# Bulk loads of four batches in two parts of uneven row counts

## The chip, the cores and the metric

One core of one Trainium2 chip. The metric is the device time of one execution in microseconds; lower is better.

## The reference

An attention layer followed by a mixture of experts, all in float32. 8 batches, 8 heads, 512 local and 32 global tokens of width 64.

```python
s_g = scale * np.matmul(q_g, k_all.transpose(0, 1, 3, 2))      # global queries see all keys
out_g = np.matmul(sm(s_g), v_all)
s_ll = np.where(np.abs(pos[:, None] - pos[None, :]) <= 32, scale * q_l @ k_l^T, -1e9)
a_l = sm(concat([scale * q_l @ k_g^T, s_ll]))                  # local queries: a window and the global keys
out_l = np.matmul(a_l, concat([v_g, v_l]))
x = concat([out_g, out_l]) as 4352 rows of 512
expert_idx = argmax(xn @ en.T / tau)                           # each row goes to one of 8 experts
out[mask] = gate_w[mask] * (np.maximum(x[mask] @ w1[e], 0.0) @ w2[e])
```

(Abridged; `sm` is a softmax. `w1` is 512 x 1024 and `w2` 1024 x 512 for each expert.)

## The kernel before

**Data as it is loaded.** The host lays out the queries and keys of a batch as `qk[b]`, 128 rows of 4 x 1216 floats (`RW` = 1216): rows 0 to 63 are heads 0 to 3, rows 64 to 127 heads 4 to 7, and the four pieces `j` of a row are the head pairs. The values are `va[b]`, two head groups of 128 rows of 14 windows of 4 x 65 floats. Rows are the partitions of the on-chip tiles `raw` (two buffers, one batch each) and `vt` (six buffers, one step each).

**Steps.** The attention stage runs in 32 steps `g`, four per batch, and two more to drain; `slot(g)` emits one. A step takes 128 local queries of all heads. In one slot the code emits, in this order: the scores of step `g` (line 415, reads `raw`), the transposes of the probabilities of `g-1` (462), the masked maxima of `g` (432, VectorE), the exponentials (451, ScalarE), the values of `g-2` (477, reads `vt`), norms, and pieces of the routing (turning the rows of `x`, logits, the choice of the expert, and a scatter of the rows to DRAM, line 730, by GpSimd's queue). The global queries of a batch are done in between (512 to 575). The order on each engine is the order of the code.

**Bulk loads.** `load(b, j, k)` (259 to 264) issues one half of one piece of a batch's `raw`: 128 rows of 608 floats, 304 KB. `load_v(g, n)` (266 to 275) issues a quarter of a step's `vt`: 128 rows of up to two windows of one head group, 260 KB, or 130 KB where a step has only three windows (`VCUT`; steps 0 and 3 of a batch). All go through SyncE's queue. The loads of `vt` for step `g` are handed out in slot `g`; those of `raw` for batch `b` in slots `4b-5` to `4b-2`, two per slot (lines 862 to 868). So steps 10, 14, 18 and 22 carry the last piece (`j` = 3) of batches 3, 4, 5 and 6, which the scores of steps 12, 16, 20 and 24 are the first to read.

**Pace.** A slot's list of loads is cut in two halves that are interleaved (878 to 881). With six loads, v0 to v3 and k0, k1, the order is v0, v3, v1, k0, v2, k1. `tick(ins, part)` (245 to 250) is called at six places of a slot, behind chosen instructions of VectorE and ScalarE, and issues from the list until its share of `part`/6 is reached; each load issued there waits for that instruction (`paced`, 231 to 240):

```python
while parts and share[0] * 6 < part * share[1]:
    parts.pop(0)()
    share[0] += 1
```

The six places are the first maximum, the copy of the turned probabilities (467), three exponentials (451) and the copy of the turned rows (596).

**Expert stage.** From about 290 us on, 36 and more blocks of 128 rows go through their expert's two matrices, with the weights loaded 2048 KB at a time.

Of the kernel before, what the change touches and what calls it, by code (L numbers as in the profile page):

```python
# [33 lines left out]
P = 128  # L34
# [10 lines left out]
RW = QW + KW  # L45
NWIN = NBQ - 2
VH = D + 1
# [6 lines left out]
VCUT = (0, 3, 7, 11, NWIN)  # L54
# [45 lines left out]
def tile_kernel(ctx: ExitStack, tc: tile.TileContext, qk, va, emb, tau, wraw, cst, out):  # L100
    nc = tc.nc
# [106 lines left out]
    with ExitStack() as actx:  # L208
# [14 lines left out]
        GW = 96 * GCUT  # L223
        assert KW - GCUT * P == GW
        half = (slice(0, D), slice(D, P))
        state = {}

        def bank():
# [2 lines left out]
        def paced(ins):  # L231

            if "mark" in state:
                tc.add_manual_dep(
                    ins.ins,
                    state["mark"].ins.name,
                    mybir.DependencyInfo(mybir.DependencyClass.Sync, mybir.DependencyReason.DATA),
                    reason="pace",
                )
            return ins  # L240
# [18 lines left out]
        def load(b, j, k):  # L259

            if ("raw", b) not in state:
                state["raw", b] = io.tile([P, 4, RS], F32, name="raw")
            lo, hi = k * RW // 2, (k + 1) * RW // 2
            paced(nc.sync.dma_start(state["raw", b][:, j, lo:hi], qk[b, :, j * RW + lo : j * RW + hi]))

        def load_v(g, n, m=2):

            b, s = divmod(g, 4)
            nw = VCUT[s + 1] - VCUT[s]
            if ("v", g) not in state:  # L270
                state["v", g] = vio.tile([P, 2, VS], F32, name="vt")
            grp, w = n % 2, n // 2 * m
            lo, hi = w * 4 * VH, min(w + m, nw) * 4 * VH
            c = VCUT[s] * 4 * VH
            paced(nc.sync.dma_start(state["v", g][:, grp, lo:hi], va[b, grp, :, c + lo : c + hi]))

        def vals(b, w, grp, j):

# [20 lines left out]
        nc.sync.dma_start(mask, cst[:, 0:MW])  # L299
        first_step(1)  # L300
        load_v(0, 0, 4)
        load_v(0, 1, 4)
        first_step(2)

# [478 lines left out]
        for g in range(NSTEP):  # L783
            b, s = divmod(g, 4)
# [10 lines left out]
        for b in range(NB):  # L795
# [4 lines left out]
            for part in range(3):  # L800
                g = 4 * b + (2 + part // 2 if b else 4)
# [57 lines left out]
        def later(g, f, *args):  # L859
            loads[g].append(lambda: f(*args))  # L860

        for g in range(1, NSTEP):
            for n in range(4):
                later(min(g, NSTEP - 2), load_v, g, n)
        for b in range(1, NB):
            for j in range(4):
                for k in range(2):
                    later(max(4 * b - 5 + j, 0), load, b, j, k)
        for n in range(EARLY + 2):
            later(4 + n, first_fill, n)  # L870

# [6 lines left out]
        for g in loads:  # L878
            n = len(loads[g])
            h = (n + 1) // 2  # L880
# [462 lines left out]
```

## Time and profile before

| what | us |
| --- | --- |
| median of 3 runs | 764.11 |
| lowest, highest | 758.47, 765.99 |
| the profiled execution | 762.38 |
| its span, first to last instruction | 760.6 |

The rows below come from the profiled execution. Its times are counted from the start of the span, and 1.8 us of the execution lie outside it. The attention stage fills the first 250 us, the expert stage the time from about 290 us on.

### The profile page before, as it was taken

The page shows a single profiled execution, that of the slowest core. Times are in us where ns is not written, and L with a number is a line of the kernel's source. Part 1 is how long each engine was busy: PE and PEld are TensorE (multiplying, and loading weights), DVE is VectorE, ACT ScalarE, POOL GpSimd, SP SyncE. Part 2 cuts the span into 40 slices and gives each one's busy share as a digit, 9 for nine tenths or more (in the row PEclk, how much of TensorE's full clock was granted, in tenths as well). Part 3 has the DMA queues.
Part 4 walks back from the last instruction along what each step waited for, and adds up shares of the span by engine and source line. Part 5 has one row for each costly group of instructions (what it writes and reads, how often), then busy time and mean ns, then how long its engine had stood idle before and what let it go on. Part 6 is the DMA issues. An engine that isn't in the chain of part 4 may idle for free.

```text
span 760.6 us, 23859 instructions
## 1 busy us (share of the span) xinstructions
PE 687.3 (90%) x8125; PEld 540.4 (71%) x8125; DVE 430.1 (57%) x1457; ACT 459.2 (60%) x956; POOL 268.7 (35%) x306
## 2 busy tenths in 40 slices
PE   9788778778767987999999999999999999999992
PEld 5576567666656545888888888888888888888881
DVE  3667777687775675454554554545454545544441
ACT  4665667657756353566666565656666666666661
POOL 1001231221211443444444444444444444445451
PEclk9999899999999998999999999999999999999996
DMA  8978978868977156464656565656565665566561
GB/s 264 329 209 231 272 229 270 266 196 281 306 232 250 65 216 237 160 251 169 251 170 246 173 241 181 236 182 234 186 217 192 224 202 209 203 208 212 200 224 65
DMA packets 66303, 165.17 MB, mean 217 GB/s; under 512 B 6516, under 2 KB 14580, under 8 KB 66176
## 3 DMA queue, kind: packets, MB, share of 16 engines
q1 hardware_dynamic: 60416, 145.67, 57.6%
q0 software_dynamic: 5760, 17.87, 6.8%
q8 instruction: 73, 1.20, 0.6%
q14 instruction: 54, 0.44, 0.2%
HBM read 142.49 MB, written 22.07 MB: 216 GB/s over the span
## 4 chain that ended last, share of the span: by engine, by line
PE 80%; issue 7%; DMA 4%; DVE 4%; ACT 2%; SPq 1%; POOL 1%; DVEq 0%; POOLq 0%
PE g L1148 18%; PE g L1143 18%; PE g L1144 18%; PE s_ps L415 4%; PE hps L1166 4%; PE po L477 4%; PE pt L462 4%; DMA raw<-in_qk_dram 3%; PE xps L1119 2%; PE pt L592 2%; PE pt L560 2%; PE po L323 1%; PE pt L512 1%; ACT pb L451 1%; PE pt L617 1%
## 5 line engine op out<-in xcount | busy, mean ns | idle before, releaser
L1139 DVE TENSOR_TENSOR WL<-stg,WH 128x512 f32 (+1 forms) x144 | 150.9, 1048 | 125.0 <-ACT WH L1137 125.0
L1139 POOL TENSOR_TENSOR WL<-stg,WH 128x512 f32 (+1 forms) x144 | 173.8, 1207 | 94.6 <-ACT WH L1137 93.7
L1137 ACT CAST WH<-stg 128x512 f32 (+1 forms) x288 | 177.4, 618 | 7.1 <-DMA stg<-in_wraw_dram 2.9
L1148 PE MATMUL g<-WH,xL 128*128 (+1 forms) x288 | 115.4, 401 | 5.3 <-DVE ob L139 5.3
L1143 PE MATMUL g<-WH,hH 128*128 (+1 forms) x288 | 120.0, 417 | 0.0
L1143 PE MATMUL g<-WH,xH 128*128 (+1 forms) x288 | 118.3, 411 | 0.0
L1144 PE MATMUL g<-WL,xH 128*128 (+1 forms) x288 | 114.9, 399 | 0.0
L1144 PE MATMUL g<-WL,hH 128*128 (+1 forms) x288 | 114.0, 396 | 0.0
L140 POOL DMA_INDIRECT out_dram<-ob x37 | 36.7, 991 | 159.6 <-ACT ob L138 145.5
L451 ACT ACTIVATE pb<-pb,nm 128x128 f32<-128x128 f32 x256 | 80.1, 395 | 11.0 <-DVE nm L432 11.0
L1169 DVE TENSOR_TENSOR hL<-hps,hH 128x512 fp32r<-128x512 f32 x72 | 49.8, 692 | 64.1 <-ACT hH L1168 64.1
L1148 PE MATMUL g<-WH,hL 128*128 (+1 forms) x288 | 84.7, 396 | 0.0
L432 DVE CUSTOM_DVE_ANT_0 pb<-s_ps,mask 128x128 f32<-128x128 f32 x256 | 56.7, 286 | 27.2 <-PE s_ps L415 26.9
L1148 PEld LDWEIGHTS g<-WH,xL 128*128 128x128 f32 x288 | 54.6, 190 | 18.8 <-DVE ob L139 5.7
L415 PE MATMUL s_ps<-raw 64*32 64x128 f32 x2048 | 47.5, 286 | 20.8 <-issue 12.8
L1160 ACT ACTIVATE h<-g 128x512 f32<-128x512 f32 x72 | 42.9, 596 | 38.3 <-PE g L1148 38.3
L1148 PEld LDWEIGHTS g<-WH,hL 128*128 128x128 f32 x288 | 54.4, 189 | 13.1
L1143 PEld LDWEIGHTS g<-WH,xH 128*128 128x128 f32 x288 | 54.9, 190 | 12.1 <-issue 0.2
L1144 PEld LDWEIGHTS g<-WL,xH 128*128 128x128 f32 x288 | 54.9, 191 | 11.9 <-issue 0.2
L138 ACT ACTIVATE ob<-g,xr 128x512 f32<-128x512 f32 x36 | 24.7, 687 | 61.2 <-PE g L1148 61.2
L1144 PEld LDWEIGHTS g<-WL,hH 128*128 128x128 f32 x288 | 54.4, 189 | 10.0
L1143 PEld LDWEIGHTS g<-WH,hH 128*128 128x128 f32 x288 | 54.3, 189 | 9.7
(198 smaller groups left out, 957.6 us busy)
## 6 DMA issues: line engine op xcount, KB each, us to landing
stg<-in_wraw_dram SPq DMA_DIRECT2D x36, 2048.0 KB
vt<-in_va_dram SPq DMA_DIRECT2D x94, 260.0 KB
raw<-in_qk_dram SPq DMA_DIRECT2D x56, 304.0 KB
xr<-xs SPq DMA_DIRECT2D x38, 257.0 KB
stg<-in_wraw_dram SPq DMA_DIRECT2D x16, 256.0 KB
vt<-in_va_dram SPq DMA_DIRECT2D x30, 130.0 KB
xs<-fill SPq DMA_DIRECT2D x12, 257.0 KB
stg<-in_wraw_dram SPq DMA_DIRECT2D x4, 512.0 KB
```

Source lines behind the costliest of these rows:

```text
L140: nc.gpsimd.indirect_dma_start(out=out[:, :], out_offset=bass.IndirectOffsetOnAxis(ap=ob[:, DM : DM + 1].bitcast(U32), axis=0), in_=ob[:, ...
L415: nc.tensor.matmul(ps[32 * j : 32 * j + 32, grp, k * P : (k + 1) * P], raw[hs, j, i * BQ : (i + 1) * BQ], raw[hs, j, c0 : c0 + P], start=True,
L432: ins = nc.vector.tensor_tensor_reduce(state["pb", g][grp][:, cs], ps[:, grp, cs], mask[:, m : m + P], -ISQ, 3.0e38, ALU.add, ALU.min, nm[ ...
L451: ins = nc.scalar.activation(pb[:, cs], pb[:, cs], AF.Exp, bias=nm[:, n : n + 1], scale=-1.0)
L462: nc.tensor.transpose(pt[:, k * P : (k + 1) * P], pb[:, k * P : (k + 1) * P], ident)
L1137: made.append(nc.scalar.copy(WH[:, ds(ra, 1), cs], s3))
L1139: made.append(eng.tensor_tensor(WL[:, ds(r, 1), cs], s3, WH[:, ds(r, 1), cs], ALU.subtract))
L1143: reads.append(nc.tensor.matmul(o.unsqueeze(1), a, WH2[:, ds(rp, 1), sl], start=first, stop=False))
L1144: reads.append(nc.tensor.matmul(o.unsqueeze(1), a, WL2[:, ds(rp, 1), sl], start=False, stop=False))
L1148: reads.append(nc.tensor.matmul(o.unsqueeze(1), a, WH2[:, ds(rp, 1), sl], start=False, stop=last))
L1160: nc.scalar.activation(h[:, nh * 512 : (nh + 1) * 512], g, AF.Relu)
L1169: nc.vector.tensor_tensor(hL[:, nh * 4 : nh * 4 + 4, :].rearrange("p c n -> p (c n)"), hp_, hv, ALU.subtract)
```

## The change

For values and for queries and keys, the bulk loads that fall into steps of batches 2 to 5 are cut by rows. `ROWS` gives the rows of the main transfers: 120 while batch 2 runs, 126 for 3, 108 for 4, 121 for 5. (`raw` of batch `b` is loaded while batch `b-1` runs, hence `ROWS[b - 1]`.) The remaining 8, 2, 20 or 7 rows come in transfers of their own: one per step for `vt` (`load_v_rest`, both head groups and all windows of the step), one per batch for `raw` (`load_rest`, all four pieces). These are 16 and 4 transfers more. They stand behind the main loads of the same kind in the slot's list before it is interleaved: `load_v_rest(g)` in slot `g`, `load_rest(b)` in slot `4b-5`. All other loads stay at 128 rows, and the bytes are the same.

```diff
+        ROWS = (P, P, 120, 126, 108, 121, P, P)
...
-            paced(nc.sync.dma_start(state["raw", b][:, j, lo:hi], qk[b, :, j * RW + lo : j * RW + hi]))
+            rows = slice(0, ROWS[b - 1])
+            paced(nc.sync.dma_start(state["raw", b][rows, j, lo:hi], qk[b, rows, j * RW + lo : j * RW + hi]))
+
+        def load_rest(b):
+
+            rows = slice(ROWS[b - 1], P)
+            paced(
+                nc.sync.dma_start(state["raw", b][rows, :, :RW], qk[b, rows, :].rearrange("p (h n) -> p h n", h=4))
+            )
...
-            paced(nc.sync.dma_start(state["v", g][:, grp, lo:hi], va[b, grp, :, c + lo : c + hi]))
+            rows = slice(0, ROWS[b])
+            paced(nc.sync.dma_start(state["v", g][rows, grp, lo:hi], va[b, grp, rows, c + lo : c + hi]))
+
+        def load_v_rest(g):
+
+            b, s = divmod(g, 4)
+            rows = slice(ROWS[b], P)
+            c, n = VCUT[s] * 4 * VH, (VCUT[s + 1] - VCUT[s]) * 4 * VH
+            paced(
+                nc.sync.dma_start(state["v", g][rows, :, :n], va[b, :, rows, c : c + n].rearrange("g p n -> p g n"))
+            )
...
+            if ROWS[g // 4] < P:
+                later(g, load_v_rest, g)
...
+            if ROWS[b - 1] < P:
+                later(4 * b - 5, load_rest, b)
```

## Rows read from the trace of the kernel before

**Rows 1.** Busy time by stretch: batches 2, 3, 4 and 5 (from the first scores of one to those of the next), then most of the expert stage. Columns: from:to in us, length, then busy us and count of PE, PEld, DVE, ACT and POOL, the granted clock, the DMA engines' share, GB/s.

```profile
58.05:86.80 28.75, 23.58 (x726) 18.65 (x725) 21.44 (x132) 19.42 (x54) 6.25 (x13) 0.94 0.88 258
86.80:120.05 33.25, 24.88 (x727) 20.06 (x726) 22.23 (x132) 20.57 (x56) 5.91 (x13) 0.90 0.83 245
120.05:149.03 28.98, 23.81 (x731) 19.12 (x730) 21.49 (x131) 20.77 (x56) 6.29 (x13) 0.94 0.83 253
149.03:178.81 29.78, 24.77 (x737) 19.05 (x736) 26.42 (x166) 18.32 (x53) 7.05 (x15) 0.94 0.74 237
...
306.00:745.00 439.00, 439.00 (x2101) 357.32 (x2100) 219.49 (x281) 275.81 (x490) 203.39 (x175) 1.00 0.60 209
```

**Rows 2.** The chain that ended last, around the starts of steps 12 and 24: start, us, what.

```profile
82.51 7.77 DMA raw<-in_qk_dram
...
175.06 6.08 DMA raw<-in_qk_dram
```

**Rows 3.** Waits from 58 to 182 us: who waited on which line, for what, us in total, times, longest. First the engines' (a `vt` load is not among those that TensorE waited for), then SyncE's queue's.

```profile
PE s_ps L415 <- DMA raw<-in_qk_dram: 5.2, 2, 3.2
...
SPq L275 <- DVE nm L432: 46.5, 16, 6.7
SPq L275 <- ACT pb L451: 17.8, 35, 1.8
...
SPq L275 <- DMA vt<-in_va_dram: 1.0, 1, 1.0
```

**Rows 4.** TensorE's timeline at the starts of steps 12, 16 and 20, and the second part of the scores of step 24: start, us, line, what, and in brackets the idle time before and its end. Steps 12 and 16 with the transposes and values behind them.

```profile
86.80 0.44 PE L415 MATMUL s_ps<-raw 64*32 64x128 f32 x12
90.41 2.20 PE L415 MATMUL s_ps<-raw 64*32 64x128 f32 x52 [3.17 <-DMA raw<-in_qk_dram]
92.54 1.97 PE L462 MATMUL pt<-ident,pb 128*128 128x128 f32 x8
94.43 1.96 PE L477 MATMUL po<-vt,pT 128*32 128x65 f32 x64
...
120.05 1.41 PE L415 MATMUL s_ps<-raw 64*32 64x128 f32 x64
121.39 1.09 PE L462 MATMUL pt<-ident,pb 128*128 128x128 f32 x8
122.41 1.12 PE L477 MATMUL po<-vt,pT 128*32 128x65 f32 x64
...
149.03 1.16 PE L415 MATMUL s_ps<-raw 64*32 64x128 f32 x64
...
181.27 1.62 PE L415 MATMUL s_ps<-raw 64*32 64x128 f32 x52 [2.02 <-DMA raw<-in_qk_dram]
```

**Rows 5.** Busy time by stretches of 2 us, columns as in rows 1.

```profile
78.00:80.00 2.00, 0.77 (x37) 0.67 (x37) 1.08 (x12) 2.00 (x7) 1.47 (x4) 1.00 1.02 386
...
86.00:88.00 2.00, 1.24 (x19) 0.59 (x17) 1.84 (x10) 2.00 (x7) 0.00 (x0) 1.00 1.12 203
...
90.00:92.00 2.00, 1.56 (x45) 1.14 (x51) 0.00 (x0) 0.17 (x1) 0.00 (x0) 0.50 1.03 382
...
116.00:118.00 2.00, 1.24 (x67) 1.03 (x68) 1.42 (x14) 1.97 (x6) 0.00 (x0) 1.00 1.01 295
```

**Rows 6.** SyncE's timeline: the last two issues of steps 10 and 14, the last of step 18, the last of step 21 and, of step 22, the first three in one row and the last two (start, us, line, what).

```profile
81.37 1.04 SPq L275 DMA_DIRECT2D vt<-in_va_dram  x1
82.51 0.45 SPq L264 DMA_DIRECT2D raw<-in_qk_dram  x1
...
113.12 0.38 SPq L275 DMA_DIRECT2D vt<-in_va_dram  x1
113.79 0.33 SPq L264 DMA_DIRECT2D raw<-in_qk_dram  x1
...
142.23 0.33 SPq L264 DMA_DIRECT2D raw<-in_qk_dram  x1
...
167.00 0.36 SPq L264 DMA_DIRECT2D raw<-in_qk_dram  x1
170.46 2.70 SPq L275 DMA_DIRECT2D vt<-in_va_dram  x3
...
174.59 0.33 SPq L275 DMA_DIRECT2D vt<-in_va_dram  x1
175.06 0.77 SPq L264 DMA_DIRECT2D raw<-in_qk_dram  x1
```

**Rows 7.** The DMA view of the stretches of rows 1: GpSimd's queue (the scatters) in batch 2, 3, 4 and 5, with packets, MB and its share of the 16 engines' time; then two sizes of the bulk loads.

```profile
q0 software_dynamic: 302, 1.01, 9.2%
...
q0 software_dynamic: 338, 1.09, 10.1%
...
q0 software_dynamic: 320, 1.05, 9.9%
...
q0 software_dynamic: 400, 1.32, 12.4%
...
vt<-in_va_dram SPq DMA_DIRECT2D x12, 260.0 KB
raw<-in_qk_dram SPq DMA_DIRECT2D x7, 304.0 KB
```

**Rows 8.** The values' matmuls (line 477), 58 to 190 us: the semaphore waits in TensorE's load queue (ns lowest, median, highest; first and last start).

```profile
L477 PEldq EVENT_SEMAPHORE  x7: 51/51/51, 75.6 to 175.1; - x7
```

## The prediction

> **What bounds the kernel now.** I read the share of busy time by stage first. The expert stage (306 to 745 us) has TensorE busy all of its 439 us, and none of the changed loads falls there [rows 1]. The change touches batches 2 to 5 of the attention stage, 58 to 179 us: four stretches of 28.75, 33.25, 28.98 and 29.78 us, in which no engine is full (PE 75 to 83%), but the DMA engines are busy 74 to 88% [rows 1]. So the stage is a loop in which engines hand work to each other, with transfers that arrive just in time.
>
> Next the chain of work that ended last. In this stretch it runs over TensorE and ScalarE except in two places: from the issue of a `raw` load at 82.51 us for 7.77 us, and from one at 175.06 us for 6.08 us [rows 2]. These are the last loads (head pair 3, second half) of the next batch's queries and keys. The waits agree: TensorE stood for `raw` twice, 5.2 us in all, and the values' matmuls waited for no `vt` load at all [rows 3]. The timeline shows where: the scores of steps 12 and 24 stop before their last 52 matmuls, for 3.17 and 2.02 us; those of steps 16 and 20 run through [rows 4].
>
> One thing more stands there. After such a stop the granted clock is 0.50, the lower of its two levels (90 to 92 us), and work that takes 1.09 and 1.12 us behind step 16 (transposes, values) takes 1.97 and 1.96 us behind step 12 [rows 4, 5]. With the 52 score matmuls (2.20 us, against 52/64 of 1.16 us) a stop of this length costs about 3.0 us more than itself.
>
> Last, SyncE's queue: an issue is 0.33 us, and it mostly waits for its pace marks on DVE and ACT, for a landing only 1.0 us [rows 3, 6]. It has room for more issues.
>
> **What the change costs.** A batch's bulk is 8 raw loads of 304 KB and value loads of 2 x 1040 + 2 x 780 = 3640 KB (two steps of four windows, two of three) [rows 7]: 6.22 MB. Where the queue was full, the 16 engines moved 386 GB/s [rows 5], 24.1 GB/s each, so a batch is 16.1 us of all of them: 8 rows of 128 per engine.
>
> *How many engines.* No row shows a bulk load of other than 128 rows, so I bound it. The cheap end: the parts still spread over 16 engines and nothing is dearer. The dear end: a transfer is dealt in equal whole rows, so 120 rows make 15 shares of 8, 126 make 14 of 9, 108 make 12 of 9, 121 make 11 of 11, and the small parts fall on engines that also carry the large one (8 by 1 row, 2 by 1, 10 by 2, 7 by 1). I take the dear end, because 128 = 16 x 8 is the only deal in which this stage's rates were reached. The busiest engine then has 9, 10, 11 and 12 rows in place of 8.
>
> [...]
>
> *The mean load.* 16.1 us times 9/8, 10/8, 11/8, 12/8 is 18.1, 20.1, 22.1 and 24.2 us. The scatters took 9.2, 10.1, 9.9 and 12.4% of the four stretches [rows 7]: 2.6, 3.4, 2.9 and 3.7 us. Together 20.7, 23.5, 25.0 and 27.9 us, against 28.75, 33.25, 28.98 and 29.78. No batch becomes bound by its busiest engine on the mean, but the last has only 1.9 us left. What remains is lateness within a step.
>
> *The critical step of each batch* (10, 14, 18, 22: four 260 KB value loads of 0.69 us, two 304 KB raw loads of 0.81 us, 4.38 us in all). Before, the last raw half is sixth of six, issued on the sixth pace mark. After, the step has seven transfers: the list is halved and interleaved, which gives v0, value rest, v1, k0, v2, k1, v3. So the last raw half moves one mark forward (to where v2 stood: 1.14, 0.67 and 0.47 us earlier in steps 10, 14 and 22 [rows 6]), and v3 goes behind it. Ahead of its end stand now 3.69 us times 8/8, 9/8, 9/8, 11/8 plus the value rest of 1, 1, 2, 1 rows of 8.3 KB (0.35 us each): 4.04, 4.50, 4.84 and 5.42 us, so -0.34, +0.12, +0.46 and +1.04 us against 4.38. To that comes backlog from the step before, at most its own growth (+0.35, +0.90, +1.24, +1.99 us), and nothing if the queue ran dry.
>
> - Step 12: -0.34, and up to +0.35 of backlog since the queue is full from 78 us [rows 5]. I take 0. Bounds -1.5 (the earlier issue counts) to +0.35.
> - Step 16: nothing is waited for, and 120.05 us is 6.26 us after the last issue at 113.79, about the 6.08 to 7.77 us that the two late ones took [rows 2, 4, 6]. So no margin: +0.12 and half of the backlog, +0.6. Bounds 0 to +1.0, and +3.0 if the clock falls.
> - Step 20: 6.80 us after the issue at 142.23, a margin of up to 0.7. +0.46 is hidden by it: 0. If the backlog comes whole, +1.0 and the clock's 3.0.
> - Step 24: +1.04; 3.46 us lie between the last issue of the step before and its own first (167.00 to 170.46 [rows 6]), which is most of a drained queue, so I add 0.3 of backlog: +1.3. Bounds +0.6 to +3.0.
>
> *Value loads.* v3 now comes last in a step, and the busiest engine is up to 2 us later. They are used two steps on: v of step 14 was last issued at 113.12 and used at 122.41 [rows 4, 6], 9.3 us for a latency of some 6 to 8. Cost 0, as no wait for `vt` stands there; if a step's cover is gone, 1 to 2 us each.
>
> *Twenty more transfers* (16 value rests, 4 raw rests): 20 x 0.33 us of SyncE, hidden under its waits for marks, the two longest of which are 64 of the 124 us [rows 3]. TensorE gets up to 20 more semaphore waits of 51 ns in its load queue [rows 8]: 0 to 1.0 us, I take 0.5.
>
> Sum: 0 + 0.6 + 0 + 1.3 + 0.5 = **+2.4 us**. Bounds of this case: -0.9 to about +12 (both clock falls and whole backlogs). The profiled execution took 762.38 us, its span 760.6; the median is 764.11. So 764.8 beside the profiled one, **766.5** beside the median. What is lost before 180 us is not given back, as the attention stage has no slack and the expert stage follows with TensorE full [rows 1].
>
> **Rivals.**
> *A. The queue becomes the bound (slower).* Place: batches 4 and 5. It decides when the busiest engine's work passes the batch's time, 6% above what I reckon for batch 5. Mechanism: the odd shares also run slower per engine. For it: full stretches also show 295 GB/s at share 1.01 [rows 5], 292 GB/s. At that rate a batch is 21.3 us; 24.0, 26.6, 29.3, 31.9 with the factors, 26.6, 30.0, 32.2 and 35.6 with the scatters: 3.2 and 5.8 us over in batches 4 and 5. With the 2.4 us, +11.4: **775.5**. Against it: 386 and 382 GB/s stand beside it, so 295 holds scatters and waits, not a ceiling. At its far end, the worst stretch (203 GB/s at 1.12), 16.1 us become 34.3, the four batches 38.6, 42.9, 47.2 and 51.5 with the factors, and with the scatters 72 us longer in all: 836.
> [...]
>
> *B. The change does not do what it says:* 16 engines whatever the rows. Then the earlier issue is left, at most -1.5 us at step 12 and -0.8 at 24, against 0.5 for the waits: **762.5**.
>
> *C. Faster.* If both stops vanished (3.17 and 2.02 us), so would the clock's price behind them (3.0 us, and at least the 0.7 of step 24's scores): 8.9 us, **755**. But step 12 needs 3.2 us and the new order gives 1.5 at most, and step 24 carries 11 rows per engine.
>
> **Chances.** Mine 0.44, A at 775.5 0.28, A's far end 0.07, B 0.15, C 0.06. 1% is 7.6 us, about what a measurement of this kernel can tell from no change. Slower by over 1% (771.8 and up): A, its far end and the tail of mine (0.04): 0.38, as a little of A stays under. Faster: 0.04 out of C. Within 1%: 0.58. The range leaves out A's far end, its upper part and most of C: 759 to 780; my own case alone is 763.2 to 776.
>
> **What would show it.** Right: bulk loads in the DMA view in two sizes; steps 12 and 24 still stop on `raw`, step 24 longer than 2.0 us; step 16 with a stop under 1 us and the clock up; the DMA share of batches 4 and 5 about as before, since it is a mean over 16 engines of which some idle. Wrong: waits for `vt` before the values, stops at every step of batches 4 and 5, or SyncE waiting for landings by tens of us (A); stops of steps 12 and 24 shorter than before (B, C).

## The result and the profile after

The changed kernel takes 769.32 us (median of 17 runs, 764.69 to 774.42), the kernel before 762.66 on the same chip (17 runs, 757.0 to 769.0). The ratio is 1.0108, 95% interval 1.0079 to 1.0136: about 8.2 us slower, 6.0 to 10.4 (the two medians differ by 6.7). The profiled execution took 769.24 us, its span 767.5. Two executions of the runs below, one with 126 rows (2296.58 us) and one of the raw halves first (1670.52), took over twice the time of all others and are left out of ratios and medians.

Busy time of the changed kernel by the stretches of [rows 1], columns as there:

```profile
57.31:92.60 35.29, 27.41 (x727) 21.42 (x726) 22.11 (x132) 20.05 (x55) 6.04 (x13) 0.81 0.84 231
92.60:122.05 29.45, 24.12 (x726) 18.82 (x725) 20.99 (x131) 19.18 (x53) 6.02 (x13) 0.94 0.80 235
122.05:154.47 32.42, 27.26 (x731) 20.46 (x730) 21.70 (x132) 20.09 (x55) 6.04 (x13) 0.89 0.75 235
154.47:189.49 35.02, 25.64 (x737) 20.39 (x736) 27.01 (x167) 20.72 (x57) 7.04 (x15) 0.90 0.73 209
```
```profile
306.00:745.00 439.00, 439.00 (x2101) 357.29 (x2100) 219.37 (x280) 275.44 (x490) 204.05 (x175) 1.00 0.60 207
```

The four batches take 132.18 us in place of 120.76 in this pair of executions, 11.4 us more, while the whole executions differ by 6.9 (769.24 less 762.38): the rest of the program took less time in this one. The expert stage is as full as before. DVE, ACT and POOL work as long as before, and the DMA share of every stretch is lower or nearly the same although the time is longer. The loads are there in two sizes. In batch 3, by the DMA view (transfers, KB each):

```profile
vt<-in_va_dram SPq DMA_DIRECT2D x12, 255.9 KB
...
vt<-in_va_dram SPq DMA_DIRECT2D x2, 16.2 KB
```

The chain around steps 12 to 24 [rows 2] goes over other loads now: no `raw`, but three `vt` loads (start, us, what).

```profile
122.25 4.97 DMA vt<-in_va_dram
154.45 5.23 DMA vt<-in_va_dram
189.34 7.70 DMA vt<-in_va_dram
```

TensorE's waits from 55 to 200 us (line, for what, us, times, longest), which answer to [rows 3]; in this wider window the kernel before stood the same 5.2 us for `raw`:

```profile
PE pt L579 <- issue: 7.2, 4, 4.5
PE s_ps L434 <- issue: 6.1, 11, 2.2
PE po L496 <- issue: 5.5, 6, 2.0
PE pt L481 <- issue: 3.7, 2, 3.4
PE pt L579 <- DMA vt<-in_va_dram: 3.2, 3, 1.3
PE pt L579 <- ACT pb L470: 2.3, 1, 2.3
PE s_ps L434 <- DMA raw<-in_qk_dram: 2.1, 2, 1.5
```

And SyncE's queue in the same time, where before it stood 1.0 us for a landing:

```profile
SPq L285 <- DMA raw<-in_qk_dram: 3.6, 3, 2.3
SPq L285 <- DMA vt<-in_va_dram: 3.6, 6, 1.2
SPq L266 <- DMA raw<-in_qk_dram: 3.1, 3, 1.4
...
SPq L266 <- DMA vt<-in_va_dram: 1.4, 2, 0.8
```

With smaller ones the landings come to 13.7 us. TensorE's stops on `raw` fell from 5.2 to 2.1 us, and stops on `vt` came, 3.2 us, on line 579: not the values of the local queries (496) but those of the global queries (`g_values`), as the timeline shows (columns as in [rows 4]; a third stop, of 1.23 us, is at 159.72):

```profile
92.60 1.16 PE L434 MATMUL s_ps<-raw 64*32 64x128 f32 x64
...
123.02 1.06 PE L434 MATMUL s_ps<-raw 64*32 64x128 f32 x52 [0.53 <-DMA raw<-in_qk_dram]
...
127.36 0.32 PE L579 MATMUL pt<-vt,gT 128*32 128x65 f32 x8 [0.63 <-DMA vt<-in_va_dram]
...
191.45 1.06 PE L434 MATMUL s_ps<-raw 64*32 64x128 f32 x52 [1.52 <-DMA raw<-in_qk_dram]
...
197.18 0.32 PE L579 MATMUL pt<-vt,gT 128*32 128x65 f32 x8 [1.32 <-DMA vt<-in_va_dram]
```

Step 12 runs through, step 16 stops for 0.53 us, step 24 for 1.52. In step 12, which now starts at 92.60 us, the granted clock is 1.00, where before it fell to 0.50 [rows 5] (the traces of both kernels have no other values than 1.00 and 0.50):

```profile
92.00:94.00 2.00, 2.00 (x74) 1.63 (x72) 1.13 (x6) 1.48 (x5) 0.00 (x0) 1.00 0.88 248
```

So in this pair what the prediction looked at, the `raw` stops, got shorter, and the time still got longer. How much shorter a single trace can't say: a second trace of the kernel before (below) stops on `raw` for 3.0 us in all.

### The profile page after: what moved, and what is told of

It is laid out like the page before. It is cut to its first block, busy times and chain, and to the rows that moved or that the text cites. A ratio compares the mean times of both kernels' runs of the same rounds, so it can differ in the third digit from the quotient of the medians.

```text
span 767.5 us, 23875 instructions
## 1 busy us (share of the span) xinstructions
PE 696.6 (91%) x8123; PEld 544.4 (71%) x8125; DVE 429.5 (56%) x1457; ACT 459.3 (60%) x956; POOL 268.5 (35%) x306
## 3 DMA queue, kind: packets, MB, share of 16 engines
q1 hardware_dynamic: 59819, 145.67, 58.0%
## 4 chain that ended last, share of the span: by engine, by line
PE 80%; issue 6%; DMA 5%; DVE 3%; ACT 3%; SPq 1%; POOL 0%; DVEq 0%; POOLq 0%; ACTq 0%
PE g L1171 18%; PE g L1167 17%; PE g L1166 17%; PE hps L1189 4%; PE s_ps L434 4%; PE po L496 4%; PE pt L481 3%; DMA raw<-in_qk_dram 2%; DMA vt<-in_va_dram 2%; PE xps L1142 2%; PE pt L611 2%; ACT pb L470 2%; PE pt L579 2%; PE pt L531 1%; PE pt L557 1%
## 5 line engine op out<-in xcount | busy, mean ns | idle before, releaser
L470 ACT ACTIVATE pb<-pb,nm 128x128 f32<-128x128 f32 x256 | 80.0, 395 | 10.6 <-DVE nm L451 10.4
L434 PE MATMUL s_ps<-raw 64*32 64x128 f32 x2048 | 50.2, 298 | 12.5 <-issue 9.2
```

Of the source, the lines that this page charges most:

```text
L434: nc.tensor.matmul(ps[32 * j : 32 * j + 32, grp, k * P : (k + 1) * P], raw[hs, j, i * BQ : (i + 1) * BQ], raw[hs, j, c0 : c0 + P], start=True,
L470: ins = nc.scalar.activation(pb[:, cs], pb[:, cs], AF.Exp, bias=nm[:, n : n + 1], scale=-1.0)
```

## The experiments

Theories at the start: the loss is (1) the twenty more transfers, (2) the new issue order, (3) fewer engines per transfer, or (4) dearer rows. In the first expectations these are N (number, 1), O (order, 2) and D (deal, 3). In the later ones E says that only the count of engines matters, S that shares which begin on every eighth row get in each other's way. Diffs are against the changed kernel unless said otherwise. Ratios are to the kernel before on the same chip.

**The order alone.** All loads at 128 rows; only empty places stand in the lists where the rests stood, so the main loads are issued at the marks of the changed kernel.

```diff
-        ROWS = (P, P, 120, 126, 108, 121, P, P)
+        ROWS = (P,) * 8
+        REST = range(2, 6)
...
-            if ROWS[g // 4] < P:
-                later(g, load_v_rest, g)
+            if g // 4 in REST:
+                later(g, int)
...
-            if ROWS[b - 1] < P:
-                later(4 * b - 5, load_rest, b)
+            if b - 1 in REST:
+                later(4 * b - 5, int)
```

> All loads at 128 rows and no small transfers; only the list of a step has the empty places that the small ones had, so the loads are issued at the pace marks of the changed kernel. Theories: D (deal), parts of 120, 126, 108 and 121 rows run on 15, 14, 12 and 11 engines and so land later; O (order), the new place of the loads in a step's list, value loads later and raw loads earlier, makes the loss; N (number), the 20 more transfers and their semaphores make it. D and N expect no loss here, a ratio of 0.995 to 1.003 to the kernel before (about 759 to 765 us), and shorter stops on raw at steps 12 and 24 than 5.2 us. O expects most of the loss of the changed kernel, 1.007 to 1.012.

0.9979 [0.9961, 0.9997], 754.0 us against 755.56. The order costs nothing; it gains 0.2%, and theory 2 falls. SyncE waits for no landing, and the four batches take 115.42 us:

```profile
57.36:172.78 115.42, 93.34 (x2917) 74.56 (x2916) 91.19 (x560) 78.61 (x215) 25.38 (x54) 0.96 0.81 257
```

**All 16 engines, uneven rows.** 112 and 16 rows in all four batches.

```diff
-        ROWS = (P, P, 120, 126, 108, 121, P, P)
+        ROWS = (P, P, 112, 112, 112, 112, P, P)
```

> Parts of 112 and 16 rows in all four batches: the same number of transfers in the same order as in the changed kernel, but both row counts divide by 16. D expects each transfer on 16 engines and no loss, 0.997 to 1.004 (760 to 766 us). N expects the loss of the changed kernel, 1.007 to 1.012, and so does O, if e1 shows it too.

1.0168 [1.0138, 1.0199], 767.43 us: with 16 shares to a transfer (by the packet counts below), where D expected no loss, it loses more than the change does. Theory 3 alone falls. The stretch is at a higher DMA share than any other, at fewer GB/s:

```profile
58.62:183.59 124.97, 96.86 (x2917) 76.60 (x2916) 91.19 (x559) 78.07 (x215) 25.29 (x54) 0.93 0.93 237
```

**The change in the old order.** Each rest is issued right behind the first main load of its kind, so the main loads keep the places they had before.

```diff
+            if (j, k) == (0, 0) and ROWS[b - 1] < P:
+                load_rest(b)
...
+            if n == 0 and ROWS[b] < P:
+                load_v_rest(g)
...
-            if ROWS[g // 4] < P:
-                later(g, load_v_rest, g)
...
-            if ROWS[b - 1] < P:
-                later(4 * b - 5, load_rest, b)
```

> The parts of the changed kernel (120, 126, 108, 121 rows and their rests), but each rest is issued right behind the first main load of its kind, so all main loads keep the places of the kernel before in a step's list. D expects the loss to stay or grow, 1.008 to 1.014 (768 to 773 us), with longer stops on raw at steps 12 to 24 than the changed kernel, since the last raw half is at the end of the step again. O expects it to go: 0.998 to 1.003. N expects 1.007 to 1.012.

1.0184 [1.0153, 1.0215], 768.15 us. That is above what any of the three expected. So the new order hides some 0.75% of a loss that is larger (0.76 plus or minus 0.42, by the two intervals). The stops without it, 55 to 200 us:

```profile
PE s_ps L438 <- DMA raw<-in_qk_dram: 7.2, 4, 2.2
PE pt L583 <- DMA vt<-in_va_dram: 7.1, 3, 3.5
```

**The kernel before once more**, unchanged, for the spread of one trace.

> The kernel before once more, for a second trace to tell what differs from one execution to the next: 757 to 769 us, stops on raw at steps 12 and 24 of 3 to 6 us in all, TensorE's waits without a releaser in the attention stage within a few us of those of the first trace.

753.48 us, span 751.6. The execution is below the 757 us that were expected, and the four batches take 115.15 us, against 120.76 in the first trace, with no edit. Step 12 stops here for 1.44 us, in place of 3.17, and the mean granted clock of the four batches is 1.00 (first row as in [rows 4], second as in [rows 1]):

```profile
88.16 1.06 PE L415 MATMUL s_ps<-raw 64*32 64x128 f32 x52 [1.44 <-DMA raw<-in_qk_dram]
```
```profile
58.20:173.35 115.15, 89.92 (x2916) 71.68 (x2915) 91.23 (x559) 78.44 (x216) 25.21 (x54) 1.00 0.81 258
```

So a difference of some 6 us between two single traces says nothing, and only the timed ratios size a part.

**As many transfers, all of 128 rows.** The extra transfer takes the last columns instead of the last rows.

```diff
+            hi -= 64 * (k == 1 and b - 1 in REST)
...
+            c = slice(RW - 64, RW)
+            paced(nc.sync.dma_start(state["raw", b][:, :, c], qk[b].rearrange("p (h n) -> p h n", h=4)[:, :, c]))
...
+            hi -= 2 * VH * (n > 1 and b in REST)
...
+            m = n - 2 * VH
+            paced(nc.sync.dma_start(state["v", g][:, :, m:n], va[b, :, :, c + m : c + n].rearrange("g p n -> p g n")))
```

> As many transfers as in the changed kernel, in its order, but all of 128 rows: the extra transfer of a step takes the last 130 columns of each head group, that of a batch the last 64 columns of each piece. [...] N expects 1.007 to 1.015. E and S expect 0.996 to 1.003 (752 to 758 us beside 755.6).

1.0009 [0.9985, 1.0033], 758.34 us against 758.07. The kernel before is not to be told from it, though SyncE's queue carries 20524 packets in the stretch in place of 13916 (rows below). As a cause of the loss theory 1 falls. But this kernel also has the order that gains 0.21%: beside the order alone, twenty more transfers cost 0.3%, plus or minus 0.3. What rows other than 128 cost is then the change less this run, 1.08 - 0.09 = some 1.0%.

**Each cut in all four batches**, to size the four parts of the change. Only the `ROWS` line differs: 120, 126, 121 and 108 rows.

```diff
-        ROWS = (P, P, 120, 126, 108, 121, P, P)
+        ROWS = (P, P, 120, 120, 120, 120, P, P)
```

> Parts of 120 and 8 rows in all four batches: 15 engines with 8 rows each, so by the number of engines the mildest of the changed kernel's cuts (busiest engine 9 rows for 8). E expects 1.000 to 1.005. [...]

> Parts of 126 and 2 rows in all four batches: 14 engines with 9 rows each. E expects more loss than for 120 and 8 (busiest engine 10 rows for 8): 1.004 to 1.010. [...]

> Parts of 121 and 7 rows in all four batches: 11 engines with 11 rows each, the strongest cut by engines (busiest engine 12 rows for 8, 27.9 of 29.8 us of a batch). E expects the largest loss of all, 1.015 to 1.030. [...]

> Parts of 108 and 20 rows in all four batches: 12 shares of 9 rows, 10 of 2; busiest engine 11 rows for 8. If the four cuts of the changed kernel add up, each for its one batch, a quarter of the losses of 120 (1.0149), 126 (1.0039), 121 (1.0127) and of this one make 1.0108, so this one is 1.012. S alone expects a mild loss, 1.003 to 1.008 (shares of 9 rows); E alone 1.008 to 1.013, between 126 and 121.

120: 1.0149 [1.0104, 1.0194], 767.72 us. 126: 1.0039 [1.0006, 1.0072], 759.82. 121: 1.0127 [1.0084, 1.0169], 765.53. 108: 1.0122 [1.0079, 1.0165], 764.01 (the last against 755.15, the others against 758.07). A quarter of each, added, is 0.0109; the change measured 0.0108. So its parts add up, and if a cut costs the same in each batch, a batch's share is a quarter: 2.8 us for 120 rows, 0.7 for 126, 2.3 for 108 and 2.4 for 121, each plus or minus 0.6 to 0.9. Only 126 rows stand apart by their interval; 15, 12 and 11 engines can't be told from each other. So the number of engines does not order these: 14 lose least, with 15 and 12 on either side. E had 1.000 to 1.005 for 120 rows and missed; S put it with 112 and 16 rows, 1.010 to 1.018 and fewer GB/s, and both came (255 GB/s against 295, below). For 126 E had 1.004 to 1.010 and S 1.000 to 1.006, and for 121 both had a range beside the 1.0127: 1.015 to 1.030 and 1.005 to 1.012.

**Thirteen engines, 8 or 9 rows each**: 104 and 24 rows, 117 and 11. As many engines by the packet counts below, shares of another length.

```diff
-        ROWS = (P, P, 120, 126, 108, 121, P, P)
+        ROWS = (P, P, 104, 104, 104, 104, P, P)
```

(and 117 in the same place)

> Parts of 104 and 24 rows in all four batches: 13 shares of 8 rows, and 12 of 2. The busiest engine has 10 rows for 8, as in the next run. S (shares that begin on every eighth row meet each other) expects a loss like 120 and 8 or more, 1.012 to 1.022. E (number of engines, rows of the busiest) expects the same as the next run, between 126 (14 engines, 1.004) and 121 (11 engines, 1.013): 1.005 to 1.010 for both.

> Parts of 117 and 11 rows in all four batches: 13 shares of 9 rows, and 11 of 1. The busiest engine has 10 rows for 8, and 13 engines run, as for 104 and 24. S expects a mild loss like 126 and 2, 1.002 to 1.008, clearly under that of 104 and 24. E expects the same as 104 and 24.

1.0142 [1.0096, 1.0189] and 1.0136 [1.0088, 1.0183], 764.91 and 766.21 us. They can't be told apart, and 117 is over the 1.002 to 1.008 of S, so S falls as what tells the cuts apart; E's equality holds, but both lose more than the 1.005 to 1.010 that it gave.

**Raw halves first**, an edit of the kernel before: in steps 2, 6, ..., 26 the two last raw halves lead the list.

```diff
+            if g % 4 == 2 and g < NSTEP - 2:
+                loads[g] = loads[g][4:6] + loads[g][:4] + loads[g][6:]
+                continue
```

> The kernel before, all loads of 128 rows, with one change of order: in the steps that carry the last piece of a batch's raw (2, 6, 10 and so on to 26) the two raw halves stand first in the list, on the first two pace marks, ahead of the value loads. If the stops on raw at the first step of each batch and the lower clock behind them are what the attention stage can still give, 0.990 to 0.997 and no wait of TensorE for raw in steps 12 to 24; if they are covered by other waits, 0.998 to 1.002.

0.9973 [0.9942, 1.0003], 752.27 us against 755.15: between its two expectations, and not told from no change for certain, though no stop on `raw` is left in the four batches. With 0.9979 of the order alone these are the best two seen.

**What all of them show of the queue.** The packets of SyncE's queue in the whole changed kernel, by the page (packets, MB, share of the 16 engines' time). Among them are packets of 4 bytes, 4703 in this trace and 4856 in the kernel before's. Counted as one for each share of a transfer, with as many shares as the largest divisor of its rows up to 16, they give the totals of these kernels:

```profile
q1 hardware_dynamic: 59819, 145.67, 58.0%
```

Before it is 60416 packets. So counted, per batch: 24 main transfers have 15, 14, 12 or 11 shares in place of 16, together 24 x 12 = 288 packets fewer; five rests add 5 x (8 + 2 + 10 + 7) = 135 (4856 - 288 + 135 = 4703); and a rest has a row's data in longer packets (148 each of 3120, 4160 and 4864 bytes, in place of 444 of 2080, 148 of 1040 and 296 of 2432), so each rest row needs 12 packets fewer, 12 x 37 = 444. 60416 - 288 + 135 - 444 = 59819, the number on the page. The seven other cuts agree with it to the packet as well (112: 59968, 120: 60096, 126: 60168, 117: 59820, 104: 59216, 108: 59272, 121: 59740).

The packets under way at once, by their starts and durations in the two traces, agree. While this queue has any, the commonest number before is 16 in each of the four stretches of [rows 1], for 15 to 18% of the time. In the changed kernel it is 15 in batch 2 (17%, with 16 for 16%), 14 in batch 3 (24%), 12 in batch 4 (30%) and 11 in batch 5 (33%). Which engine takes which share stands in no trace.

Now the same queue in the four batches alone, by the DMA view of that stretch of each kernel: the kernel before and its second trace, then columns (128 rows), 126, 117, 104, 108, 121, 120 and 112 rows, and the changed kernel.

```profile
q1 hardware_dynamic: 13916, 25.04, 70.3%
```
```profile
q1 hardware_dynamic: 13810, 24.84, 68.8%
```
```profile
q1 hardware_dynamic: 20524, 25.46, 71.3%
```
```profile
q1 hardware_dynamic: 13760, 25.17, 70.4%
```
```profile
q1 hardware_dynamic: 13128, 24.62, 69.8%
```
```profile
q1 hardware_dynamic: 12691, 24.90, 69.0%
```
```profile
q1 hardware_dynamic: 12891, 25.19, 65.7%
```
```profile
q1 hardware_dynamic: 13264, 25.04, 63.6%
```
```profile
q1 hardware_dynamic: 13871, 25.54, 77.4%
```
```profile
q1 hardware_dynamic: 13288, 24.68, 81.4%
```
```profile
q1 hardware_dynamic: 13385, 25.11, 67.2%
```

MB over share and length is the rate of 16 engines while they work on this queue: before 25.04 MB / (0.703 x 120.76 us) = 295 GB/s, and 313 in the second trace of the same kernel. The share times the rows of the busiest engine over 8, plus the scatters' share (9.5 to 10.5%), is an estimate of how full that engine is, with the shares as counted; that the rests fall on engines that carry the main part is assumed, and no run shows it. The ns are the median time of one packet of 2080 bytes (a row of a 260 KB value load), from the packets in the same stretch of each trace.

| rows | engines | busiest engine's rows / 8 | stretch, us | GB/s | ns per row | busiest engine, estimate | ratio |
| --- | --- | --- | --- | --- | --- | --- | --- |
| 128 (before) | 16 | 8/8 | 120.76 | 295 | 85 | 0.81 | |
| 128 (before, second trace) | 16 | 8/8 | 115.15 | 313 | 85 | 0.80 | |
| 128, by columns | 16 | 8/8 | 119.31 | 299 | 85 | 0.82 | 1.0009 |
| 112 + 16 | 16, 16 | 8/8 | 124.97 | 243 | 116 | 0.92 | 1.0168 |
| 120 + 8 | 15, 8 | 9/8 | 129.29 | 255 | 107 | 0.97 | 1.0149 |
| 126 + 2 | 14, 2 | 10/8 | 121.61 | 294 | 85 | 0.98 | 1.0039 |
| 117 + 11 | 13, 11 | 10/8 | 121.78 | 290 | 86 | 0.97 | 1.0136 |
| 104 + 24 | 13, 12 | 10/8 | 125.63 | 287 | 92 | 0.96 | 1.0142 |
| 108 + 20 | 12, 10 | 11/8 | 127.78 | 300 | 88 | 1.00 | 1.0122 |
| 121 + 7 | 11, 7 | 12/8 | 126.16 | 312 | 86 | 1.05 | 1.0127 |

(Shares can pass 1: so they stand in [rows 5].) The reader sees two prices. In the uniform cuts to 16 and 15 engines the rows are dearer, 243 and 255 GB/s; with 14 to 11 the rate is near that of 128 rows (287 to 312 against 295 to 313), but fewer engines carry the bytes. The packets show the first price directly: 85 ns at 128 rows, 116 and 107 at 112 and 120. (The four batches of the changed kernel, 120, 126, 108 and 121 rows in one trace, have 264, 287, 306 and 279 GB/s, and 85, 85, 92 and 106 ns: single stretches do not sort the rows in the same way.) It is not only that 16 engines run at once: with 16 packets under way in the middle of a row's time, the median row took 85 ns before and 119 at 112 rows. Nor is it the longer packets of the rests: 104 + 24 has more of them, and 92 ns. Either way the busiest engine goes from some 0.8 to 0.92 and more, and the slack in which a late transfer caught up is gone (this last is argued). So theories 3 and 4 can each hold for some of the cuts, and neither for all. And 126 + 2 does not fit its place: as full by this estimate, a third of the loss. A full engine is then not enough for a loss, and that it is what costs the time at 121 to 104 rows is argued, not shown. At 126 rows only two of 14 engines reach 10 rows by this estimate and the others have 9; whether that is the reason was not tried, nor main parts and rests apart.

Why the rows are dearer at 112 and 120 no run here shows. Where shares begin, on every eighth row at 104 and every ninth at 117, had no effect on the time that shows: 1.0142 and 1.0136.

## Why the prediction was partly right

769.32 us is in the range, between the main case (+2.4 us, 766.5) and rival A (+11.4, 775.5); the loss is 8.2, nearer to A's than to the main case's, and at 1.08% just over the 1% to which it gave a chance of 0.38. So the range held, and it was wide; the size and place of the loss were not foreseen. By batch, from the four uniform cuts:

| rows | predicted at | us | a quarter of the uniform cut, us |
| --- | --- | --- | --- |
| 120 (batch 2) | step 12 | 0 | 2.8 |
| 126 (batch 3) | step 16 | +0.6 | 0.7 |
| 108 (batch 4) | step 20 | 0 | 2.3 |
| 121 (batch 5) | step 24 | +1.3 | 2.4 |
| 20 transfers | TensorE's waits | +0.5 | not told from 0 or from 0.5 (0.3% beside the order alone, plus or minus 0.3) |

- *The deal* was right in the number of shares, and B with it out: by the packet counts 15, 14, 12 and 11 for the 16 of 128 rows, and as many packets under way. That the small parts fall on engines that carry the large one, so that the busiest has 9 to 12 rows in place of 8, no run shows; the factors 9/8 to 12/8 remain an estimate.
- *The last raw half moves forward*: right in sign. The order alone gains 0.2%, and with odd rows it saves 0.75%. Step 16 stops 0.53 us (0.6 was said, and the clock stayed at 1.00). But step 12, which was to stop as before, has no stop, and step 24 was to stop 2.02 + 1.3 us and stopped 1.52. In this trace both fell on the side that was named as wrong, although the kernel is slower: the loss is not at the place where it was looked for. Steps 12 and 24 of the second trace of the kernel before stop for 1.44 and 1.57 us, so the 3.17 and 2.02 that the prediction built on, and the clock's price of 3.0 us, are of one execution.
- *The mean load* is the step that failed. It took the 386 GB/s of the best 2-us row for the rate of a loaded queue, 16.1 us per batch. The stage's own mean, by the rows above, was 295 before the change, and 313 in the second trace. At 295, 6.22 MB are 21.1 us, the busiest engines have by the estimate 23.7, 26.4, 29.0 and 31.6, and with the scatters 26.3, 29.8, 31.9 and 35.3 us. The changed kernel took 35.29, 29.45, 32.42 and 35.02, so that batches 3 to 5 lie at their busiest engine; at 313 the sums are 1.4 to 1.8 us less. Without either rate, the changed kernel's own shares of this queue (74.8, 68.1, 65.1 and 60.6%), taken as in the table, give 0.93, 0.95, 0.98 and 1.02 for the busiest engine of batches 2 to 5. "No batch becomes bound by its busiest engine on the mean" was therefore wrong for batches 4 and 5 by this estimate, as rival A has it, whose 32.2 and 35.6 come from nearly the same rate. That the full engine is what cost the time stays open, as 126 + 2 shows. Batch 2 is not explained so. Its row shows 0.81 of the clock and a gap of 4.53 us that the profile puts down to nothing but "issue" (below); the timed 120 rows cost 2.8 us, and 9 us of this trace are beyond that model.
- Rival A's *mechanism* was half right. In the uniform cuts odd shares run slower per engine at 112 and 120 rows (243, 255 GB/s), not at 108 and 121 (300, 312). Its rate, 292 to 295, was about right since 128 rows ran at 295 too. (B's own terms give 762.3 us, not 762.5.)
- *The chain* was read wrongly: from 58 to 182 us it runs over VectorE too, 51 pieces of 10.9 us in all, among them most of 154.6 to 160.9 us and of 165.6 to 169.8 in batch 5. The sum has no term for it. Two of its rows:

```profile
155.61 0.69 DVE xt L493
...
166.66 0.69 DVE xt L493
```

- *"Value loads. Cost 0"* failed: the step looked at the values of the local queries alone, two steps behind the load. `g_values` of a batch runs from the first step of the next and reads the `vt` of the step just before: 0.63, 1.23 and 1.32 us of stops, where before there was none. The chain's three `vt` rows are these. The order alone has no such stop and the columns 0.3 us, so it takes the uneven rows.
- *SyncE "has room for more issues"*: for issues, yes (columns: 0.3 us for landings). But it waits 13.7 us for landings, between the 1.0 of before and A's tens; in the uniform cuts it is 8 to 23, 3.9 with 126 rows, none in the order alone. That sorts the mild cut from the others better than the engine's fullness, but as a sign, not a cause.
- *The DMA share "about as before"*: right in batch 5 (0.73 against 0.74), lower in batch 4 (0.75 against 0.83). The mean over 16 engines does hide the loss, as said.

Where the 11.4 us between the two traces went, by TensorE's rows from 55 to 200 us and the two stretches: raw -3.1, `vt` +3.2, "issue" 22.5 less 17.8 = +4.7, and 104.43 less 97.05 = 7.4 us more of TensorE's own busy time at a mean clock of 0.88 in place of 0.93. But two traces of one kernel, before, differ by as much: 115.15 and 120.76 us, 89.92 and 97.05 us of TensorE's busy time at a mean clock of 1.00 and 0.93, with 19.4 and 17.8 us of "issue". So this split is a picture of one pair and not a measurement of 8.2, and what the clock has to do with the loss is not shown. What stays open: why rows at 112 and 120 are dearer, why 126 + 2 is mild, and through which waits the loss reaches the end.

## What to carry to other kernels

Take the rate of a loaded queue from the whole stage (MB over share and time of that queue), not from its best 2 us, and multiply by the busiest engine's rows: mean DMA shares of 0.73 to 0.84 went here with an estimated 0.93 to 1.02 of the busiest engine; take it from more than one trace, as one kernel gave 295 and 313. Cut bulk loads by columns and keep 128 rows; with rows off 128, even 112 in 16 shares, the same bytes cost 1.2 to 1.7% here (0.4% at 126), while twenty more transfers of 128 rows cost 0.3% plus or minus 0.3. Before a cover is counted on, list every reader of the buffer, the rare ones too.

## What the hardware showed unexpectedly

Loads of 112 rows in 16 shares ran at 243 GB/s, with 116 ns for the median row, where 128 rows ran at 295 to 313 and 85 ns. The cut with 2 rows on the side (126 + 2) was nearly free, those with 7 to 24 were not. And TensorE stood 17.8 us before and 22.5 us after, of 145, for nothing that the profile names; over all the kernels it is 14.1 to 28.4, with no order by loss. Of the kernel before, 55 to 200 us:

```profile
PE po L477 <- issue: 7.5, 6, 2.0
PE s_ps L415 <- issue: 6.0, 4, 2.9
...
PE pt L560 <- issue: 3.1, 2, 2.9
```

and the longest of the changed kernel, in the chain of batch 2 (start, us, what):

```profile
61.13 4.53 issue
```

The queue of the instructions themselves moved 0.38 MB over the same DMA engines in the four batches, 1.2% of their time, in both kernels. That these gaps wait for such packets is a guess that no run here separates.
